# Weight, input and constant loads moved between the groups' transposing transfers, and four weight splits queued behind a normalisation chain

## The chip, the cores and the metric

The kernel runs on one core of a Trainium2 chip. A core has five engines, each with its own queue of instructions that it takes strictly in order: TensorE (PE, matrix products; its weight loads appear as PEld), VectorE (DVE), ScalarE (ACT), GpSimd (POOL) and SyncE (SP), which here only issues DMA transfers. All transfers of this kernel are issued by SP and share 16 DMA engines. The metric is the device time of one execution in microseconds (us), as the median of several runs. The profile shows one further execution; its times are counted from the start of its span.

## The reference

The input x has 2048 rows (tokens) of 448 features, in float32. The output is the sum of three things:

```python
xn  = layernorm(x)
out = x + A(xn) + B(xn)

def A(x):                       # a filter in the frequency domain
    return irfft2(rfft2(x) * (w_r + 1j * w_i))

def B(x):                       # token shift, then a channel MLP
    h  = gelu(layernorm(x) @ w1)             # w1: 448 x 448
    hs = shift(h) @ w2                       # four quarters of the features, shifted
    x1 = x + hs                              #   by +1, -1, +2, -2 tokens; w2: 448 x 448
    return x1 + gelu(layernorm(x1) @ w3) @ w4   # w3: 448 x 1792, w4: 1792 x 448
```

## The kernel before

Matrix products in float32 precision are made of float16 halves: a number is split into a high half (written by ACT) and a low half (the rest, written by DVE), and a product takes three passes (high by high, high by low, low by high). The weights are scaled first by a power of two that is worked out from the sum of their squares (`squares` on ACT, `powers` on PE and DVE), and then split (`split_w`, lines 258-261).

**Tokens.** The 2048 tokens lie in 16 blocks of 128 rows; block b holds every sixteenth token, so that a shift by a token is a step to the neighbouring block. The blocks are worked in four groups of four: `GRP = [[14, 15, 0, 1], [2, 3, 4, 5], [6, 7, 8, 9], [10, 11, 12, 13]]`. In this document they are the first to the fourth group (g = 0 to 3 in the code).

**The first stage**, up to about 115 us, does for each group, in this order:

- `load_x(g)` (line 190): two transfers of 448 KB bring the group's x.
- `norm1(g)` (lines 292-344): DVE takes statistics of the four blocks, then a chain of small DVE instructions gives scale and bias (the last of them writes `nm`, line 306), then the four blocks are scaled, each by POOL, ACT or DVE as the list `apply` says.
- `T1(g)` (line 741, `transpose_split` at 356): PE transposes the blocks with 16 products, ACT and DVE write the halves `xT`.
- `w1_unit` (408), four times: 11 products with w1, GELU on ACT, high half `hs` on ACT (line 417), low half on DVE (line 418), and a *transposing DMA* from SP (line 421) that writes the block's `h` with features on partitions. The buffers `hs` are four, used in turn (for the fourth group three), so that the halves of the next group can be written only when the transposing transfers of the group before have read theirs.
- `w2_tile(b)` (425), four times: 12 products of `h` with w2. Tile b takes `h` of the blocks b-1, b+1, b-2 and b+2, so that it needs blocks of the neighbouring groups too. The products with w2's low half need what DVE writes at line 260.
- `ln2` (442): the second normalisation of pairs or fours of blocks. It ends with a transposing DMA of its own (line 473) into `x2mem`.

**The second stage** (`mlp`): `front` multiplies with w3 (22 products of 256 columns each), ACT and DVE make halves `hf`; `back` multiplies them with w4 into `acc`. The first `mlp([0])` starts while the last tiles of the first stage run; the frequency filter (lines 870-909) runs beside the others. The matrices `w3raw` (four parts of 896 KB, the last part in two transfers of 448 KB to 64 partitions each) and `w4raw` (four transfers, inside `x2mem`) are needed for their squares, and then for their splits. The constants `csm` (643 KB) are first read by the filter's products at line 523.

**What sets the order.** The program text gives dependencies and wishes; a planner of the framework, when the kernel is built, lays down the order of each engine's queue. `with behind(key)` (line 349) tells the planner that an instruction is to be issued after those remembered in `after[key]`: `("h", g, i)` is the transposing DMA of block i of group g, `("a1",)` the last halves of the second group's transposition, `("a2",)` those of the third's. A further rule of the framework concerns SP: each DMA also waits until the eighth DMA before it has landed.

The order of SP's queue in the first stage of the kernel before: x of the first group, w1, x of the second, w2, x of the third and the fourth, all of w3, csm; then the four transposing transfers of the first group, four of the second, four loads of w4, four of the third group, four transfers of line 473, four of the fourth group.

Of the kernel before, what the change touches and what calls it, by code (L numbers as in the profile page):

```python
# [16 lines left out]
ALU = mybir.AluOpType  # L17
# [102 lines left out]
def body(tc, nc, x, wf, w1, w2, w3, w4, c_g, c_n, c_small, out):  # L120
    V, A, P, T, SY = nc.vector, nc.scalar, nc.gpsimd, nc.tensor, nc.sync
# [28 lines left out]
    def bank(tag, name):  # L150
        return ps.tile([128, 512], F32, tag=tag, bufs=2, name=name)
# [38 lines left out]
    def load_x(g):  # L190
        for b0 in sorted(GRP[g])[::2]:
            SY.dma_start(xt[b0 // 2], xv[:, b0:b0 + 2])
# [8 lines left out]

    load_x(1)
    SY.dma_start(w2s[:112], w2.rearrange("(k p) n -> p k n", p=112))
    for g in (2, 3):
        load_x(g)
    w3raw = pa.tile([128, 4, F], F32, tag="R", bufs=1, name="w3raw")

    def load_w3(ts):
        for t in ts:
            if t < 3:  # L210
                SY.dma_start(w3raw[:, t], w3[128 * t:128 * t + 128])
            else:
                for h in range(2):
                    SY.dma_start(w3raw[64 * h:64 * h + 64, 3], w3[384:448])

    load_w3(range(4))
    x2mem = pw.tile([128, 9 * F], F16, name="x2mem")
    x2all = x2mem[:, 0:8 * F].rearrange("p (j t n) -> p j t n", j=4, t=7)
    w4raw = x2mem.bitcast(F32)[:, F:].rearrange("p (f n) -> p f n", f=14)
# [3 lines left out]
    def load_w4(i):  # L223
        SY.dma_start(w4raw[:, W4F[i]:W4F[i + 1]], w4v[:, W4F[i]:W4F[i + 1]])

    csm = pc.tile([128, 2 * (256 + 2 * DF + 452 + 128)], F16, name="csm")
# [13 lines left out]
    def powers(m, n, key, tag="acc"):  # L240

        t = pc.tile([128, 2], F32, name=f"pt{key}")
        V.tensor_reduce(out=t[:, 0:1], in_=m[:, :n], axis=AX.X, op=ALU.add)
        pm = bank(tag, f"pm{key}")
        i = T.matmul(pm[:, 0:1], ones, t[:, 0:1], start=True, stop=True)
        after["p" + key] = (i.ins,)
        V.tensor_scalar(out=t[:, 1:2], in0=pm[:, 0:1], scalar1=2.0 ** -58, scalar2=None, op0=ALU.max)
        e = pc.tile([128, 3], I32, name=f"pe{key}")
        V.tensor_scalar(out=e[:, 0:1], in0=t.bitcast(I32)[:, 1:2], scalar1=1, scalar2=0x7F800000,
                        op0=ALU.logical_shift_right, op1=ALU.bitwise_and)  # L250
        V.tensor_scalar(out=e[:, 1:2], in0=e[:, 0:1], scalar1=-1, scalar2=185 << 23, op0=ALU.mult, op1=ALU.add)
        V.tensor_scalar(out=e[:, 2:3], in0=e[:, 0:1], scalar1=1, scalar2=69 << 23, op0=ALU.mult, op1=ALU.add)
        return e.bitcast(F32)[:, 1:2], e.bitcast(F32)[:, 2:3]
# [38 lines left out]
    def norm1(g, apply):  # L292

        bs = GRP[g]
        n, b0 = len(bs), bs[0]
        mv = pc.tile([128, 4, 2], F32, name=f"mva{b0}")
        stats([xb(b) for b in bs], f"a{b0}", mv)
        a = pc.tile([128, 2 * n], F32, name=f"va{b0}")
        yi = pc.tile([128, 2 * n], I32, name=f"vy{b0}")
        y = yi.bitcast(F32)  # L300
        V.tensor_scalar(out=a[:, n:], in0=mv[:, :n, 1], scalar1=1.0 + EPS, scalar2=EPS * EPS, op0=ALU.mult, op1=ALU.add)
        V.tensor_scalar(out=a[:, 0:n], in0=mv[:, :n, 1], scalar1=EPS, scalar2=None, op0=ALU.add)
        V.tensor_single_scalar(yi, a.bitcast(I32), 1, op=ALU.logical_shift_right)
        V.tensor_scalar(out=yi, in0=yi, scalar1=-1, scalar2=0x5F3759DF, op0=ALU.mult, op1=ALU.add)
        nm = pc.tile([128, n], F32, name=f"nma{b0}")
        V.scalar_tensor_tensor(out=nm, in0=mv[:, :n, 0], scalar=-1.0, in1=y[:, n:], op0=ALU.mult, op1=ALU.mult)
        for k, b in enumerate(bs):
            y_, m_ = y[:, n + k:n + k + 1], nm[:, k:k + 1]
            if apply[k] is A:
                A.activation(out=xb(b), in_=xb(b), func=AF.Identity, scale=y_, bias=m_)  # L310
            else:
                i = apply[k].tensor_scalar(out=xb(b), in0=xb(b), scalar1=y_, scalar2=m_, op0=ALU.mult, op1=ALU.add)
                if apply[k] is V:
                    after["n", g] = (i.ins,)

        q, z = (pc.tile([128, 2 * n], F32, tag=f"v{t}", bufs=2, name=f"v{t}{b0}") for t in "qz")
        w, r = (pc.tile([128, 2 * n], F32, name=f"v{t}{b0}") for t in "wr")
        nm1 = pc.tile([128, n], F32, name=f"nm{b0}")

        def refine():  # L320
            P.tensor_tensor(out=q, in0=y, in1=y, op=ALU.mult)
            P.tensor_tensor(out=q, in0=q, in1=a, op=ALU.mult)
            P.tensor_scalar(out=w, in0=q, scalar1=-10.0 / 3.0, scalar2=None, op0=ALU.add)
            P.tensor_tensor(out=w, in0=w, in1=q, op=ALU.mult)
            P.tensor_scalar(out=w, in0=w, scalar1=5.0, scalar2=None, op0=ALU.add)
            P.tensor_tensor(out=z, in0=w, in1=w, op=ALU.mult)
            P.tensor_tensor(out=z, in0=z, in1=q, op=ALU.mult)
            P.tensor_scalar(out=z, in0=z, scalar1=-0.5 * 0.375 ** 3, scalar2=1.5 * 0.375, op0=ALU.mult, op1=ALU.add)
            P.tensor_tensor(out=r, in0=z, in1=w, op=ALU.mult)
            P.tensor_scalar(out=gsc[:, 4 * g:4 * g + 4], in0=r[:, n:], scalar1=r1, scalar2=None, op0=ALU.mult)  # L330

        def scales():
            c, r1st, u = cs[:, 4 * g:4 * g + 4], w[:, 0:n], w[:, n:]
            P.tensor_tensor(out=r1st, in0=r[:, 0:n], in1=y[:, 0:n], op=ALU.mult)
            P.tensor_tensor(out=u, in0=r[:, n:], in1=r[:, n:], op=ALU.mult)
            P.tensor_tensor(out=c, in0=y[:, n:], in1=a[:, n:], op=ALU.mult)
            P.tensor_tensor(out=c, in0=c, in1=u, op=ALU.mult)
            P.tensor_tensor(out=c, in0=c, in1=r1st, op=ALU.mult)
            P.tensor_scalar(out=c, in0=c, scalar1=s12[:, 0:1], scalar2=None, op0=ALU.mult)
            P.tensor_tensor(out=nm1, in0=mv[:, :n, 0], in1=r1st, op=ALU.mult)  # L340
            P.tensor_scalar(out=nm1, in0=nm1, scalar1=-1.0, scalar2=None, op0=ALU.mult)
            for k, b in enumerate(bs):
                xn_scale[b], xn_bias[b] = r1st[:, k:k + 1], nm1[:, k:k + 1]
        return refine, scales

    after = {}

    @contextlib.contextmanager
    def behind(*key):
        key = key if len(key) > 1 else key[0]  # L350
        with contextlib.ExitStack() as st:
            for i in after[key]:
                st.enter_context(tc.issue_after(i))
            yield
# [53 lines left out]
    def w1_unit(g, i, pm=None):  # L408
        if pm is None:
            pm = bank(("mm", "mm", "acc", "acc")[i], f"pw1_{g}{i}")  # L410
            w1_in(g, i, pm, range(4))
        c = CS[GRP[g][i]]
        pm = pm[:, :D]
        pv_ = pm.rearrange("p (k n) -> p k n", k=4)
        h = hs_buf[c % (HS if g == 3 else HS + 1)]
        A.activation(out=pm, in_=pm, func=AF.Gelu_apprx_tanh, scale=gsc[:, c:c + 1])
        u = A.activation(out=h[:, 0, :, 0:112], in_=pv_, func=AF.Copy, scale=h1)
        v = V.scalar_tensor_tensor(out=h[:, 1, :, 0:112], in0=pv_, scalar=h1, in1=h[:, 0, :, 0:112],
                                   op0=ALU.mult, op1=ALU.subtract)
        o = h_at(g, i)  # L420
        d = SY.dma_start_transpose(out=hT[g][:, :, o:o + 128], in_=h.rearrange("p i k n -> p (i k n)"))  # L421
        after[g, i] = u.ins, v.ins
        after["h", g, i] = (d.ins,)
# [356 lines left out]
        T1(1, range(2, 4))  # L780
    for k in range(4):
        w1_unit(0, k, first[k])
    n1[1][0]()
    s12 = pc.tile([128, 4], F32, name="s12")
    V.tensor_tensor(out=s12[:, 0:1], in0=h1, in1=s2, op=ALU.mult)
# [2 lines left out]
    p12, eps12 = s12[:, 1:2], s12[:, 2:3]  # L788
    with behind("a1"):
        n1.append(norm1(2, [P, V, A, P]))  # L790
    with behind("a1"):
        for k in range(4):
            split_w(w2p[:, 0, k], w2p[:, 1, k], w2s[:112, k], s2[:112])
    h_alloc(1)
# [1 line left out]
        w1_unit(1, k)  # L796
    T1(2)
    with behind("h", 1, 3):
        for i in range(4):
            load_w4(i)  # L800
    n1[2][0]()
    for n in n1:
        n[1]()
# [2 lines left out]
    h_alloc(2)  # L806
    for k in range(4):
        w1_unit(2, k)
    for k in range(4):
        with behind(*((1, 3), ("a2",), ("a2",), (2, 0))[k]):  # L810
            squares(m3[:, k:k + 1], w3raw[:, k])
    s3, r3 = powers(m3, 4, "3", "mm")
    h3 = pc.tile([128, 1], F32, name="h3")
# [17 lines left out]
    h_alloc(3)  # L831
    for k in range(4):
        w1_unit(3, k)
    s4, r4 = powers(m4, 7, "4")
    p34 = pc.tile([128, 2], F32, name="p34")
    V.scalar_tensor_tensor(out=p34[:, 1:2], in0=r3, scalar=2.0 ** 5, in1=r4, op0=ALU.mult, op1=ALU.mult)
# [17 lines left out]
    for b in range(12, 16):  # L854
        w2_tile(b)
    ln2(range(12, 16), [P, A, P, A])
    SY.dma_start(csm, c_small)
    close("p1")
    close("pr")

# [76 lines left out]
```

## Time and profile before

| What | Value |
|---|---|
| median of 3 runs | 427.64 us (427.53 to 428.42) |
| the profiled execution | 432.02 us |
| its span, from the first instruction to the last | 430.2 us |
| PE busy | 413.0 us, 96% of the span |
| DVE, ACT, POOL busy | 294.8, 249.2, 109.9 us |
| moved by DMA | 47.61 MB |

The profile names a group of instructions by the line of the kernel, the engine, the operation and the tiles (output, then inputs). Matrix products are pipelined: a product's own duration is longer than the distance from one to the next, so that PE can be shown as busy and still lose time; the number of products in a stretch, times their distance when they follow each other closely, tells more than the busy time. "SPq" is SP issuing a transfer. In a timeline, what stands in brackets is the time for which the engine sat idle before the instruction and what ended it. In a table of stretches the columns are the length, then for each engine its busy time with the number of instructions, then the granted clock of TensorE as a share of full speed, the busy share of the DMA engines and the bytes moved.

### The profile page before, as it was taken

The page shows a single profiled execution, that of the slowest core. Times are in us where ns is not written, and L with a number is a line of the kernel's source. Part 1 is how long each engine was busy: PE and PEld are TensorE (multiplying, and loading weights), DVE is VectorE, ACT ScalarE, POOL GpSimd, SP SyncE. Part 2 cuts the span into 40 slices and gives each one's busy share as a digit, 9 for nine tenths or more (in the row PEclk, how much of TensorE's full clock was granted, in tenths as well). Part 3 has the DMA queues.
Part 4 walks back from the last instruction along what each step waited for, and adds up shares of the span by engine and source line. Part 5 has one row for each costly group of instructions (what it writes and reads, how often), then busy time and mean ns, then how long its engine had stood idle before and what let it go on. Part 6 is the DMA issues. An engine that isn't in the chain of part 4 may idle for free.

```text
span 430.2 us, 8446 instructions
## 1 busy us (share of the span) xinstructions
PE 413.0 (96%) x3289; PEld 288.0 (67%) x3289; DVE 294.8 (69%) x619; ACT 249.2 (58%) x428; POOL 109.9 (26%) x191
## 2 busy tenths in 40 slices
PE   7987999999998999999999999999999999999994
PEld 3543654666657777777778888787676767576772
DVE  4885799899756567663478889865999529942211
ACT  4685598974765867553387888864544414423221
POOL 2442270100223963420022211210454203200000
PEclk9998999999999999999999999999999999999998
DMA  8999926321755337223146565520001003431001
GB/s 279 366 267 182 308 50 109 75 52 35 182 105 110 87 122 265 89 86 98 38 115 159 152 160 151 139 73 8 2 2 64 23 2 129 148 111 43 2 0 44
DMA packets 51688, 47.61 MB, mean 111 GB/s; under 512 B 33920, under 2 KB 46912, under 8 KB 51648
## 3 DMA queue, kind: packets, MB, share of 16 engines
q1 hardware_dynamic: 51648, 47.07, 41.0%
q8 instruction: 26, 0.43, 0.4%
q14 instruction: 14, 0.11, 0.1%
HBM read 35.52 MB, written 3.67 MB: 91 GB/s over the span
## 4 chain that ended last, share of the span: by engine, by line
PE 49%; DVE 20%; ACT 9%; DMA 8%; issue 7%; SPq 3%; POOL 3%; ACTq 0%; DVEq 0%; POOLq 0%
PE pw L372 20%; PE acc L696 18%; PE pw L437 4%; ACT te L602 3%; PE ps L523 2%; DMA x2mem<-y 2%; SPq L421 2%; PE pw L398 2%; DVE te L604 1%; ACT zb L613 1%; DVE w4p L260 1%; DMA xr<-x 1%; DMA out<-xr 1%; DMA w1s<-w 1%; DVE pf L588 1%
## 5 line engine op out<-in xcount | busy, mean ns | idle before, releaser
L372 PE MATMUL pw<-x2mem,w3p 128*128 128x256 f16 x1232 | 152.0, 273 | 0.0
L696 PE MATMUL acc<-w4p,hf 128*128 128x448 f16 x672 | 139.9, 352 | 2.1 <-DVE hf L684 1.5
L372 PEld LDWEIGHTS <-w3p 128*128 128x128 f16 x1232 | 118.9, 98 | 24.4 <-issue 0.9
L696 PEld LDWEIGHTS <-hf 128*128 128x128 f16 x672 | 65.1, 98 | 53.4 <-DVE hf L684 2.3
L684 DVE SCALAR_TENSOR_TENSOR hf<-pw,h,hf 128x512 f16<-128x512 f32 x56 | 41.8, 748 | 57.9 <-ACT hf L683 57.5
L681 ACT ACTIVATE pw<-pw,pe 128x512 f32<-128x512 f32 x56 | 36.7, 656 | 68.2 <-PE pw L372 67.1
L437 PE MATMUL pw<-w2p,h 112*128 112x448 f16 x192 | 41.8, 363 | 2.9 <-DMA h<-hs 2.4
L683 ACT ACTIVATE hf<-pw,h 128x512 f16<-128x512 f32 x56 | 38.4, 687 | 1.5
L398 PE MATMUL pw<-w1p,xT 128*128 128x448 f16 x176 | 34.8, 352 | 1.5 <-ACT xT L365 0.8
L606 POOL TENSOR_TENSOR z<-te 128x450 f32<-128x450 f32 x16 | 16.3, 1018 | 74.0 <-DVE te L604 74.0
L437 PEld LDWEIGHTS <-h 112*128 112x128 f16 x192 | 18.9, 100 | 20.3 <-DMA h<-hs 3.7
L398 PEld LDWEIGHTS <-xT 128*128 128x128 f16 x176 | 17.0, 98 | 17.8 <-ACT xT L365 1.1
L653 POOL TENSOR_TENSOR e<-e 128x226 f32<-128x226 f32 x16 | 13.9, 867 | 56.5 <-ACT e L650 45.3
L587 ACT ACTIVATE pf<-pp 64x450 f16<-64x450 f32 x32 | 17.3, 542 | 16.6 <-DVE pf L588 8.1
L588 DVE TENSOR_TENSOR pf<-pp,pf 64x450 f16<-64x450 f32 x32 | 19.9, 622 | 5.3 <-ACT pf L587 5.0
L650 ACT ACTIVATE e<-pe 128x452 f32<-128x452 f32 x16 | 8.7, 548 | 15.6 <-DVE vh L661 12.3
L602 ACT ACTIVATE te<-px 64x450 f32<-64x450 f32 x32 | 17.3, 540 | 0.5
L660 ACT ACTIVATE vh<-e 128x448 f16<-128x448 f32 x16 | 9.2, 575 | 13.9 <-DVE e L658 8.3
L503 POOL TENSOR_TENSOR xr<-xf 128x452 f32<-128x452 f32 x8 | 9.7, 1207 | 27.0 <-issue 22.6
L506 POOL TENSOR_TENSOR f<-xr 128x452 f32<-128x452 f32 x16 | 16.1, 1029 | 0.6
L514 DVE TENSOR_TENSOR xh<-f,xh 128x452 f16<-128x452 f32 x16 | 11.8, 777 | 6.2 <-ACT xh L513 6.2
L668 PE MATMUL py<-vh,csm 128*128 128x448 f16 x48 | 13.5, 352 | 1.5 <-DVE vh L661 0.7
(155 smaller groups left out, 599.2 us busy)
## 6 DMA issues: line engine op xcount, KB each, us to landing
wc<-wf SPq DMA_DIRECT2D x32, 225.0 KB, 3.7
wl<-wf SPq DMA_DIRECT2D x8, 450.0 KB, 3.6
xt<-x SPq DMA_DIRECT2D x8, 448.0 KB, 8.1
xf<-x SPq DMA_DIRECT2D x8, 448.0 KB, 3.9
w3raw<-w SPq DMA_DIRECT2D x3, 896.0 KB, 13.6
xr<-x SPq DMA_DIRECT2D x12, 224.0 KB, 2.6
out<-xr SPq DMA_DIRECT2D x12, 224.0 KB, 1.9
gn<-c_g SPq DMA_DIRECT2D x16, 128.0 KB, 3.3
```

What stands on the lines that cost most here:

```text
L372: T.matmul(ps_out, wp[:, wi + t, cols], xT[:, xi + t, tok], start=t == 0 and wi + xi == 0, stop=t == 3 and wi == 4)
L398: T.matmul(pm[:, :D], xTs[g][:, xi + t, 128 * i:128 * i + 128], w1p[:, wi + t], start=t == 0 and wi + xi == 0, stop=t == 3 and wi == 4)
L437: T.matmul(pm[:, :D], hT[g][:112, 4 * hi + k, o:o + 128], w2p[:, wi, k], start=n == 0, stop=n == 11)
L506: P.tensor_tensor(out=f[:, :, k:k + 2].rearrange("p b s d -> p s b d"), in0=u[:, :, 0], in1=u[:, :, 1], op=op)
L587: A.activation(out=hi, in_=src, func=AF.Copy)
L588: V.tensor_tensor(out=lo, in0=src, in1=hi, op=ALU.subtract)
L602: A.activation(out=e[64 * h:64 * h + 64], in_=px_[64 - 64 * h:128 - 64 * h, :2 * DF], func=AF.Copy)
L606: P.tensor_tensor(out=z, in0=t[:, 0], in1=t[:, 1], op=ALU.add)
L681: A.activation(out=pm, in_=pm, func=AF.Gelu_apprx_tanh, scale=r3)
L683: i = A.activation(out=h[:, 0], in_=pm, func=AF.Copy, scale=h3)
L684: j = V.scalar_tensor_tensor(out=h[:, 1], in0=pm, scalar=h3, in1=h[:, 0], op0=ALU.mult, op1=ALU.subtract)
L696: m = T.matmul(acc[G][i][:, :D], h[:, hi, o:o + 128], w4p[0][:, wi, f], start=f == 0 and n == 0, stop=f == 13 and n == 2)
```

## The change

Eight places change. The order that comes out of the planner for SP's queue is then: x of the first group, w1, x of the second, w2, x of the third, the first two parts of w3; four transposing transfers of the first group; x of the fourth group, the third part of w3; four transposing transfers of the second group; the last part of w3 (two transfers), two loads of w4; four transposing transfers of the third group; two loads of w4; two transfers of line 473 and three of the fourth group; two of line 473; the last of the fourth group; csm. The work of no engine is added to or taken away, but since the planner starts from other times, the queues of PE, ACT, DVE and POOL differ up to the first products of the second MLP pass; after that all queues are in the same order as before.

```diff
-    for g in (2, 3):
-        load_x(g)
+    load_x(2)
...
-    load_w3(range(4))
+    load_w3([0, 1])
...
-        V.scalar_tensor_tensor(out=nm, in0=mv[:, :n, 0], scalar=-1.0, in1=y[:, n:], op0=ALU.mult, op1=ALU.mult)
+        i = V.scalar_tensor_tensor(out=nm, in0=mv[:, :n, 0], scalar=-1.0, in1=y[:, n:], op0=ALU.mult, op1=ALU.mult)
+        after["c", g] = (i.ins,)
...
+    with behind("h", 0, 3):
+        load_x(3)
+        load_w3([2])
...
-    with behind("a1"):
+    with behind("a1"), behind("c", 2):
         for k in range(4):
             split_w(w2p[:, 0, k], w2p[:, 1, k], w2s[:112, k], s2[:112])
...
     with behind("h", 1, 3):
-        for i in range(4):
-            load_w4(i)
+        load_w3([3])
+        load_w4(0)
+        load_w4(1)
...
+    with behind("h", 2, 3):
+        load_w4(2)
+        load_w4(3)
     for k in range(4):
-        with behind(*((1, 3), ("a2",), ("a2",), (2, 0))[k]):
+        with behind(*(("a2",), ("a2",), (2, 0), (2, 1))[k]):
             squares(m3[:, k:k + 1], w3raw[:, k])
...
+    with behind("h", 3, 3):
+        SY.dma_start(csm, c_small)
...
-    SY.dma_start(csm, c_small)
```

In the order of the changed kernel's queues, `split_w` of w2 lies as follows: its four instructions on DVE stand behind the third group's `nm`, its four on ACT stand where they stood. PE's queue has one product of the first `w2_tile` in the middle of the second group's products with w1, and it takes the third group's transposition and the first 14 of its products with w1 ahead of the first product that reads the second group's `h`; in the kernel before, that transposition lies among the first four tiles, whose products read that `h`, and the products with w1 lie behind them.

## The prediction

> **What bounds the kernel now.** I read the page first, then the table of stretches, then the timelines of PE, SP and DVE where PE loses time.
>
> ```profile
> span 430.2 us, 8446 instructions
> PE 413.0 (96%) x3289; PEld 288.0 (67%) x3289; DVE 294.8 (69%) x619; ACT 249.2 (58%) x428; POOL 109.9 (26%) x191
> ```
>
> PE is busy for 96% of the span. Since busy times of products overlap, I take their distances instead, from two dense pieces of the chain that ended last:
>
> ```profile
> 73.13 5.68 PE pw L398 x30
> 81.08 5.79 PE pw L372 x53
> ```
>
> A product of 448 columns takes 5.68/30 = 0.189 us, one of 256 columns 5.79/53 = 0.109 us. With these, the stretches in which PE loses time between 34 and 132 us are found (the first row of the table is for the loads, below):
>
> ```profile
> 0.00:20.00 20.00, 17.40 (x85) 8.66 (x85) 12.98 (x42) 10.88 (x21) 7.25 (x30) 1.00 0.94 314
> 34.00:38.50 4.50, 1.72 (x9) 0.44 (x8) 2.20 (x7) 2.82 (x5) 0.00 (x0) 1.00 1.09 215
> 38.50:42.00 3.50, 3.50 (x10) 1.46 (x11) 1.57 (x6) 2.96 (x4) 1.94 (x5) 0.52 1.13 189
> 66.00:70.00 4.00, 3.42 (x21) 1.66 (x20) 3.97 (x10) 3.09 (x5) 0.00 (x0) 1.00 0.71 133
> 125.00:132.00 7.00, 5.14 (x31) 2.62 (x30) 5.28 (x9) 3.86 (x8) 4.21 (x4) 1.00 0.52 99
> ```
>
> From 34 to 38.5 us PE issues 9 products, 9 x 0.189 = 1.7 us of work in 4.5: 2.8 lost. In the next 3.5 us the granted clock is 0.52 and 10 products (1.9 us of work) fill them: 1.6 lost. From 66 to 70 us 0.6 is lost, from 125 to 132 us 1.9. Together 6.9 us. PE's timeline names what it waited for:
>
> ```profile
> 26.11 8.12 PE L398 MATMUL pw<-w1p,xT 128*128 128x448 f16 x42 [0.25 <-DVE xT L366]
> 35.75 0.74 PE L437 MATMUL pw<-w2p,h 112*128 112x448 f16 x3 [1.52 <-DMA h<-hs]
> 38.49 4.67 PE L437 MATMUL pw<-w2p,h 112*128 112x448 f16 x15 [0.58 <-DMA h<-x2mem]
> 49.86 8.49 PE L398 MATMUL pw<-w1p,xT 128*128 128x448 f16 x44
> 86.70 1.87 PE L437 MATMUL pw<-w2p,h 112*128 112x448 f16 x9
> 128.94 0.93 PE L696 MATMUL acc<-w4p,hf 128*128 128x448 f16 x4 [0.61 <-ACT hf L683]
> 131.23 1.12 PE L696 MATMUL acc<-w4p,hf 128*128 128x448 f16 x5 [1.24 <-DVE hf L684]
> ```
>
> The first stall is for the first group's transposing transfers. Why they are late is seen at SP, in its timeline, in the landing times of the first of them alone, of all of them, and of the four loads of w4, and in the page's line of csm:
>
> ```profile
> 16.72 0.34 SPq L857 DMA_DIRECT2D csm<-c_small x1
> 23.96 11.12 SPq L421 DMA_TRANSPOSE h<-hs x3
> 42.15 2.68 SPq L224 DMA_DIRECT2D x2mem<-w x4
> ...
> DMA to landing us min/median/max: 10.8/10.8/10.8
> ...
> DMA to landing us min/median/max: 3.0/3.2/10.8
> ...
> DMA to landing us min/median/max: 5.3/8.2/10.7
> ...
> csm<-c_small SPq DMA_DIRECT2D x1, 643.0 KB, 17.2
> ```
>
> The first one, issued at 23.96, lands 10.8 us later, at 34.8, where 3.2 is the median; SP itself is held for 11 us over three issues. The loads ahead add up to 9.6 MB (8 x 448 KB of x, 784 of w1, 784 of w2, 3,584 of w3, 643 of csm), and the first 20 us move 314 GB/s: they need 31 us, and csm, the last of them, lands at 16.72 + 17.2 = 33.9. So the wait is for loads that nobody needs yet.
>
> **The first group's transfers.** In the changed order 6 x 448 + 784 + 784 + 2 x 896 KB lie ahead of them, 6.2 MB, which the first 20 us move (314 x 20 = 6.3 MB). The queue is empty when the first is issued at 23.96. It and the next two land 3.2 us after their issue, at 27 to 31 us; the fourth follows its low half on DVE (next part). PE's queue now has one product of the first tile behind 14 of the second group's (two of these lie ahead of the 42 above), so at 26.1 + 12 x 0.189 = 28.4. It needs block 15, whose transfer is issued 1.5 us after the first and lands at 28.7: 0.3 us of new stall. The second group's products then end at 34.5 (34.2 before).
>
> **DVE: w2's low halves behind the third group's chain.**
>
> ```profile
> 28.59 2.21 DVE L284 BATCH_NORM_STATS2 sta<-xt 128x6 f32<-128x448 f32 x4
> 30.71 1.27 DVE L260 SCALAR_TENSOR_TENSOR w2p<-w2s,pe,w2p 112x448 f16<-112x448 f32 x2
> 31.89 0.69 DVE L418 SCALAR_TENSOR_TENSOR x2mem<-pw,h,x2mem 128x448 f16<-128x448 f32 x1
> 35.54 0.69 DVE L418 SCALAR_TENSOR_TENSOR hs<-pw,h,hs 128x448 f16<-128x448 f32 x1 [1.49 <-ACT hs L417]
> 40.01 0.16 DVE L306 SCALAR_TENSOR_TENSOR nma<-mva,vy 128x4 f32<-128x4 f32 x1
> 34.88 0.63 ACT L417 ACTIVATE hs<-pw,h 128x448 f16<-128x448 f32 x1 [2.27 <-DMA h<-hs]
> ```
>
> Before, the chain's statistics end at 30.8, but `nm` is written at 40.2: the w2 halves stand ahead, then DVE waits for ACT, which waits for the first transposing transfer to have read its `hs` buffer. Changed: the fourth `hs` half at 30.8 to 31.4 (its transfer lands at 34.6), the chain's nine small instructions to 32.5 (0.09 to 0.2 us each), 7.7 us earlier. Then three w2 halves (0.63 each, from 1.27 for two), one block's scaling (0.5), the fourth: 35.5. What queues behind them are the second group's low halves: they start at 35.5, as before. So the second group's transfers are issued from 36.2 on, 0.7 after the first low half starts, about where they were. The delayed w2 halves are first read at about 34.8 and later; the first ends at 33.1, each further one ahead of its product.
>
> **Third group instead of waiting.** With `nm` at 32.5 its blocks are scaled by 34.9. PE has from 34.5 on: 11 products of the first group's `h`, the 16 transpositions (1.97 us for 16 by the row below) and 14 products with w1, 2.1 + 2.0 + 2.6 = 6.7 us, to 41.2, before a product needs the second group's `h`.
>
> ```profile
> 22.51 1.97 PE L362 MATMUL pta<-ident,xt 128*128 128x128 f32 x16 [0.65 <-POOL xt L312]
> ```
>
> **Loads put between.** x of the fourth group and a part of w3 (1.8 MB, 5.9 us at 314 GB/s) are queued behind the transfer that lands at 34.6 and ahead of those issued from 36.2: these land from about 41.4 on (40.5, and 0.9 for the transfer itself, as between csm and the first one). PE needs block 2 at 41.2: 0.2 to 0.3 us of stall. Bounds: 3.2 us from issue (39.4, no stall) and 10.8 (47.0, 5.8 us). I take the sum of bytes. The third group's first transfer is issued at about 47.5 (20 products after 41.4 PE has its first two blocks, at 45.2; GELU and the halves take some 2 us), lies behind 2.7 MB and lands at about 54. PE needs it 75 products and 12 transpositions after 41.4, at 57: hidden. The loads' own readers: the fourth group's x is read by DVE after the third group's `xT` halves, at about 40 (lands at 37.5); the third part of w3 by ACT after the third group's first half, at 47 (40.5); the last, two transfers of 448 KB behind the second group's, by ACT after the second half, at 50 (about 48.6); w4 and csm later, with over 5 us to spare. Each is covered by ACT's and DVE's earlier work; uncovered, ACT's queue and through it the w3 splits on DVE would move one for one.
>
> So to the middle of the stage PE gets back 2.8 + 1.6 (no gap, no half clock) + 0.6 and pays 0.3 + 0.3.
>
> **The fourth group.** Before, its first low half, the transfer and PE's use read:
>
> ```profile
> 81.55 0.66 DVE L418 SCALAR_TENSOR_TENSOR hs<-pw,h,hs 128x448 f16<-128x448 f32 x1
> 82.27 5.86 SPq L421 DMA_TRANSPOSE h<-hs x4
> ```
>
> Landing at 82.27 + 3.2 = 85.5, use at 86.70: 1.2 us in hand. In the changed queue PE has 31 instead of 53 products with w3 ahead of that use, 22 x 0.109 = 2.4 us less cover. If DVE gets there earlier by as much as PE does, PE stalls 2.4 - 1.2 = 1.2 us. DVE can: it has the same work, and between 34 and 48 us it was busy for 6.6 us only:
>
> ```profile
> 34.00:48.00 14.00, 11.22 (x57) 5.92 (x56) 6.56 (x16) 7.84 (x14) 5.20 (x20) 0.88 1.07 235
> ```
>
> **The loss at 125 to 132.** ACT reaches the `hf` half late there, because it waits in front of it for a `y` buffer that a transfer of line 473 has not yet read:
>
> ```profile
> 113.86 1.48 SPq L493 DMA_DIRECT2D xf<-x x3
> 115.64 3.98 SPq L473 DMA_TRANSPOSE x2mem<-y x2
> 122.75 0.67 ACT L459 ACTIVATE y<-xt,nm 128x448 f32<-128x448 f32 x1 [3.59 <-DMA x2mem<-y]
> ```
>
> These two transfers are queued behind three loads of x for the filter. In the changed order both pairs of line 473 go out ahead of these loads, so the 1.9 us go; late next is DVE with `hf`, for which I keep 0.5.
>
> **Sum.** Back: 2.8 + 1.6 + 0.6 + 1.9 = 6.9. Paid: 0.3 + 0.3 + 1.2 + 0.5 = 2.3. Net 4.6. After that all queues are in the old order, and PE is dense, so the shift stays. The span becomes 425.6, the execution 432.0 - 4.6 = 427.4; the runs' median stands 4.4 below the profiled execution, and I take the same difference off it: 427.64 - 4.6 = 423.0.
>
> **Rivals.**
> - *Nothing new stalls* (0.08): the whole 6.9 comes back, 420.7. Against it: the fourth group has too little cover.
> - *VectorE becomes the bound* (0.19). From 57 to 93 us it has hardly a free moment (it was 7 us idle before 48 and moves only by 4.6), and tiles wait for it to empty PSUM banks: the loss at 125 to 132 stays (1.9) and 0.5 more is lost: 425.4.
> - *Loads too late* (0.06). The last part of w3 behind the second group's transfers lands 10.7 us after its issue at 41.9, as the last of w4 did: 52.6 instead of 50. ACT, then the w3 splits and the fourth group are 2.6 later: 425.6. The Trainium skill, DMA: Bandwidth & Descriptors, Rules for kernel authors, speaks against the change here: it says to issue a DMA early and wait for it late, so that its fixed cost overlaps. The trace of before shows what early issue costs others, 10.8 us for a transfer behind the loads.
> - *Slower* (0.10). The second group's transfers, now behind loads, take 10.8 us as the first group's did: PE waits from 41.2 to 47.0, 5.8 us, and the half clock after a gap costs its 1.6 again: 423.0 - 0.3 + 5.8 + 1.6 = 430.1. It decides once they land after about 44.3, 8 us after issue (3.1 of stall and 1.6 for the clock use up the 4.6).
> - *No effect* (0.03): the stalls only move, 427.6.
>
> My forecast has 0.54. From 421 to 425 is its own range; with VectorE as the bound and the late loads the range is 420.4 to 426.4. Faster by over 0.2%, which is about what a measurement of this kernel can tell from no change (the three runs spread by 0.2%): 0.86; within it 0.04; slower 0.10.
>
> **What would show it.** The first transposing transfer lands near 27, not 34.8; no half clock near 40; the third group's products with w1 begin near 38 instead of 49.86; `nm` of that group near 32.5; the first use of the fourth group's `h` near 80 to 82, with a wait of about 1 us for DMA; no wait for `hf` near 125. Wrong would be: PE waiting over 3 us for `h` near 41, or DVE late with line 439 so that PE waits for banks between 57 and 95.

## The result, and the profile after

The changed kernel takes 426.27 us (median of 15 runs, 424.62 to 428.35), beside 428.31 for the kernel before in the same series; the ratio is 0.9945, with a 95% interval of 0.9923 to 0.9967. It is faster, by about 0.55% where 1.1% (427.64 to 423.0) was forecast; the medians differ by 2.0 us where 4.6 were forecast. 426.27 lies inside the forecast's wide range, above its own 421 to 425. The profiled execution took 428.35 us, 2.1 more than the median.

Top of the page of the changed kernel, then its table of stretches (length; busy time and instructions of PE, PEld, DVE, ACT and POOL; granted clock; DMA share; GB/s):

```profile
span 426.6 us, 8457 instructions
PE 412.9 (97%) x3289; PEld 288.1 (68%) x3289; DVE 291.7 (68%) x619; ACT 248.6 (58%) x428; POOL 107.8 (25%) x191
```

```profile
34.00:38.50 4.50, 4.34 (x27) 2.56 (x26) 4.27 (x8) 3.73 (x8) 4.07 (x8) 1.00 1.02 282
38.50:42.00 3.50, 3.50 (x23) 2.00 (x21) 3.02 (x5) 3.40 (x5) 2.15 (x11) 1.00 1.48 221
42.00:49.00 7.00, 4.82 (x18) 2.05 (x17) 3.93 (x16) 2.02 (x4) 1.79 (x5) 0.76 1.07 153
66.00:70.00 4.00, 4.00 (x23) 2.07 (x22) 4.00 (x11) 4.00 (x6) 0.00 (x0) 1.00 0.83 210
```

From 34 to 42 us PE is now nearly full. But from 42 to 49 it issues 18 instructions in 7 us, at a granted clock of 0.76: the gap and the half clock have moved some 7 us back. The timelines of DVE, PE and SP show the way there:

```profile
32.90 0.16 DVE L305 SCALAR_TENSOR_TENSOR nma<-mva,vy 128x4 f32<-128x4 f32 x1
32.98 1.87 DVE L259 SCALAR_TENSOR_TENSOR w2p<-w2s,pe,w2p 112x448 f16<-112x448 f32 x3
```

```profile
38.94 0.55 PE L398 MATMUL pw<-w1p,xT 128*128 128x448 f16 x2
...
44.38 2.51 PE L437 MATMUL pw<-w2p,h 112*128 112x448 f16 x9 [2.19 <-DMA h<-hs]
...
83.55 1.87 PE L437 MATMUL pw<-w2p,h 112*128 112x448 f16 x9
...
125.39 2.07 PE L696 MATMUL acc<-w4p,hf 128*128 128x448 f16 x10 [0.47 <-DVE hf L684]
```

```profile
24.47 4.57 SPq L421 DMA_TRANSPOSE h<-hs  x3
...
34.34 1.30 SPq L210 DMA_DIRECT2D w3raw<-w  x1
36.49 8.02 SPq L421 DMA_TRANSPOSE h<-hs  x3
```

The third group's `nm` comes at 32.90 instead of 40, its products with w1 begin at 38.94 instead of 49.86, as forecast. Then PE waits 2.19 us for the second group's `h`. The first of those transfers was issued at 36.5, behind x of the fourth group and the third part of w3; this answer on the transposing transfers issued from 35.5 to 37 us has its time from issue to landing:

```profile
DMA to landing us min/median/max: 7.8/7.8/7.8
```

The first group's first transfer, by the same view, took 3.4 us (10.8 before), as forecast. Up to here one would say: the second group's transfers took the gain back. A second profile of both kernels, below, shows that this is only half of it.

### The profile page after: what moved, and what is told of

Its sections match the earlier page's. It is cut to its first block, busy times and chain, and to the rows that moved or that the text cites. A ratio compares the mean times of both kernels' runs of the same rounds, so it can differ in the third digit from the quotient of the medians.

```text
span 426.6 us, 8457 instructions
## 1 busy us (share of the span) xinstructions
PE 412.9 (97%) x3289; PEld 288.1 (68%) x3289; DVE 291.7 (68%) x619; ACT 248.6 (58%) x428; POOL 107.8 (25%) x191
## 4 chain that ended last, share of the span: by engine, by line
PE 54%; DVE 8%; issue 3%; DMA 3%; ACT 1%; POOL 1%; DVEq 0%; SPq 0%
PE pw L372 22%; PE acc L696 22%; PE ps L523 3%; PE pu L625 2%; PE pp L580 2%; PE px L597 2%; DMA xr<-x 2%; DVE xt L669 1%; DMA out<-xr 1%; DVE xr L480 1%; DVE vh L661 1%; DVE e L657 1%; DVE x2mem L480 1%; DVE e L655 1%; DVE U L638 1%
## 5 line engine op out<-in xcount | busy, mean ns | idle before, releaser
L398 PE MATMUL pw<-w1p,xT 128*128 128x448 f16 x176 | 36.4, 360 | 1.4 <-ACT xT L365 0.8
L416 ACT ACTIVATE pw<-pw,gsc 128x448 f32<-128x448 f32 x16 | 9.3, 606 | 10.7 <-POOL xt L312 5.7
```

The costliest lines, as they stand in the source:

```text
L398: T.matmul(pm[:, :D], xTs[g][:, xi + t, 128 * i:128 * i + 128], w1p[:, wi + t], start=t == 0 and wi + xi == 0, stop=t == 3 and wi == 4)
```

## The experiments

All ratios are to the kernel before, run beside on the same chip, with 95% intervals. "Lost PE time" is the distance between the starts of successive products beyond the one that their columns need in dense stretches (0.187 us for 448 columns, 0.107 for 256), summed over a stretch of the trace. How small an excess is counted moves such a sum by up to 0.4 us, and the difference of two sums by some 0.3.

**The two halves of the change, one at a time.** First the w2 halves (the four DVE instructions that write w2's low halves) alone behind the third group's chain (the two edits below added to the kernel before, all loads where they were):

```diff
+        after["c", g] = (i.ins,)
...
-    with behind("a1"):
+    with behind("a1"), behind("c", 2):
         for k in range(4):
             split_w(...)
```

> The kernel before with one part of the change: VectorE's halves of w2 behind the third group's chain; all loads where they were. The first group's transfers still land from 34.8 on. PE's queue has the products that need them ahead of most of the third group's transposition, so it still waits from 34.2 to about 38.4, with 6 products and 2 transpositions inside; the third group's scale is there near 32.5 and its products with w1 can follow soon after 40. Theory 'the transfers are what PE waits for': ratio 0.998 to 1.002, the gap and the half clock near 38 to 42 remain. Theory 'the chain is what counts': ratio near 0.9945, as the whole change.

Measured: 423.84 us, ratio 0.9916 (0.9888 to 0.9944). The theory that the late transfers are what costs (about 1.000) fell: by its median the half that moves no load is ahead even of the whole change (0.9945), though the two intervals overlap. Its PE timeline:

```profile
35.93 0.36 PE L438 MATMUL pw<-w2p,h 112*128 112x448 f16 x1 [1.61 <-DMA h<-hs]
36.71 1.12 PE L438 MATMUL pw<-w2p,h 112*128 112x448 f16 x5 [0.42 <-DMA h<-hs]
...
80.22 1.87 PE L438 MATMUL pw<-w2p,h 112*128 112x448 f16 x9
...
124.42 0.92 PE L697 MATMUL acc<-w4p,hf 128*128 128x448 f16 x4
125.17 0.27 PE L373 MATMUL pw<-x2mem,w3p 128*128 128x256 f16 x1
125.28 1.68 PE L697 MATMUL acc<-w4p,hf 128*128 128x448 f16 x8
```

The first group's transfers are as late as before (10.3 us from issue to landing) and PE still waits for them, 1.61 and 0.42 us. But with `nm` at 32.48 the third group fills the time behind, and nothing is lost near 80 and 125. Why nothing is lost near 125 is most likely told by SP and ACT:

```profile
111.75 1.85 SPq L494 DMA_DIRECT2D xf<-x  x3
118.30 5.27 SPq L474 DMA_TRANSPOSE x2mem<-y  x4
```

```profile
113.46 0.67 ACT L460 ACTIVATE y<-xt,nm 128x448 f32<-128x448 f32 x1 [1.15 <-DMA x2mem<-y]
```

No edit touches these transfers, but the planner, which starts from other times, leaves four of the sixteen behind the filter's loads of x, where the kernel before leaves six. ACT's last wait for a `y` buffer ends at 113.46; in the kernel before it ends at 122.75, with the `hf` that is late behind it in ACT's queue. The changed kernel and all other variants have this order of SP's queue too.

Then the rest of the change alone, that is the moved loads and the later squares of w3 (the changed kernel without `behind("c", 2)`); its label and the forecast for it call this the loads alone:

> The changed kernel without the moved w2 halves: these stand ahead of the third group's chain again, the loads are as changed. The first group's transfers land from 27.9 on; the third group's scale comes near 35 instead of 33, its transposition starts near 37.5. PE waits about 1 us there, but by 42 it waits for the second group's transfers in any case. Theory 'loads are the change': ratio 0.994 to 0.998. Theory 'only both together': ratio 0.999 to 1.002.

Measured: 426.82 us, ratio 0.9972 (0.9952 to 0.9993). The w2 halves alone bring 0.84%, the rest alone 0.28%, both together 0.55% and, in a second series, 0.63%. By these figures the rest takes back some 0.2 to 0.3 points of what the w2 halves bring; since the intervals overlap, the ratios alone do not show it, and the traces have to say what is lost and where. That was the next question.

**What lies between the first and the second group's transfers.** Nothing there (x of the fourth group up front; w3's last two parts and one load of w4 behind the second group's transfers, three loads of w4 behind the third's); in part, against the changed kernel:

```diff
-    with behind("h", 0, 3):
-        load_x(3)
-        load_w3([2])
...
-        load_w3([3])
+        load_w3([2, 3])
```

> The changed kernel, but with nothing loaded between the first and the second group's transposing transfers: x of the fourth group goes in front of w3's first two parts, the third part of w3 goes behind the second group's transfers with the fourth part and one quarter of w4, the other three quarters behind the third group's. Theory 'loads between': in the changed kernel the second group's transfers land at 44.3 because x and w3 (1.8 MB) lie ahead of them, PE stands idle for 2.35 us at 42 and then runs 3.4 us at half clock (1.7 us). Without these loads the transfer issued near 36.5 lands near 39.6, PE waits at most 1 us near 39, no half clock between 30 and 60: about 3 us less than the changed kernel, ratio to before 0.986 to 0.990. Rival 'late by themselves' (the transposing transfers of the second group are slow for another reason): landing near 44 again, ratio 0.9945.

Measured: 425.54 us, ratio 0.9957 (0.9925 to 0.9989). The second group's first transfer lands at 39.2 and PE waits for none of them, yet the time is that of the changed kernel. The lost time has only moved; ACT's and PE's timelines:

```profile
48.94 1.70 ACT L238 ACTIVATE x2mem<-w3raw 128x1792 f16<-128x1792 f32 x1 [1.53 <-DMA w3raw<-w]
...
52.97 1.70 ACT L238 ACTIVATE x2mem<-w3raw 128x1792 f16<-128x1792 f32 x1 [0.67 <-DMA w3raw<-w]
```

```profile
83.39 1.88 PE L438 MATMUL pw<-w2p,h 112*128 112x448 f16 x9 [0.82 <-DMA h<-hs]
...
126.91 1.69 PE L697 MATMUL acc<-w4p,hf 128*128 128x448 f16 x8 [1.36 <-DVE hf L685]
```

ACT waits for the parts of w3, PE for the fourth group's `h` and for `hf`. The second variant exchanges the part of w3 between the transfers for a load of w4, so that two parts of w3 come later (against the changed kernel):

```diff
     with behind("h", 0, 3):
         load_x(3)
-        load_w3([2])
+        load_w4(0)
...
-        load_w3([3])
-        load_w4(0)
+        load_w3([2, 3])
```

> The changed kernel with one load swapped: between the first and the second group's transfers goes a quarter of w4 (896 KB, in rows of 1,792 bytes) instead of the third part of w3 (896 KB, in rows of 7,168 bytes); that part of w3 goes behind the second group's. Theory 'bytes': the same bytes ahead, the second group's first transfer lands near 44.3 again, the same gap of 2.35 us and the half clock, ratio 0.994 to 0.995. Theory 'slow w3 part': in the changed kernel that part took 4.8 us (38.5 to 43.3) where others took 2.2 to 2.4; if it is w3's rows that are slow beside queued transposing transfers, w4's quarter lands near 41, the transfers near 42, the gap shrinks under 1 us, no half clock: 2.5 to 3.5 us less than the changed kernel, ratio 0.986 to 0.989.

Measured: 429.18 us, ratio 1.0027 (1.0002 to 1.0052): slower than the kernel before, and outside both forecasts. Near 42 it went as the theory of the slow w3 part has it: w4's quarter lands at 41.3, the first transposing transfer at 42.1, and nothing is lost there. But in the second profile of the changed kernel (below) w3's part lands at 40.4, so its rows alone are not what made it late. ACT and PE:

```profile
50.95 1.70 ACT L237 ACTIVATE x2mem<-w3raw 128x1792 f16<-128x1792 f32 x1 [3.43 <-DMA w3raw<-w]
...
55.03 1.70 ACT L237 ACTIVATE x2mem<-w3raw 128x1792 f16<-128x1792 f32 x1 [1.28 <-DMA w3raw<-w]
```

```profile
54.62 2.24 PE L437 MATMUL pw<-w2p,h 112*128 112x448 f16 x11 [1.17 <-DVE xt L439]
```

ACT stands 3.43 us before one square of w3, with the third group's halves queued behind it, and PE loses 3.2 us between 50 and 70. So the forecast's rival "loads too late" is real when two parts of w3 come late, in a stronger form than it was given. The sentence of the Trainium skill that was set beside it (DMA: Bandwidth & Descriptors, Rules for kernel authors: issue early, wait late) fits these two runs.

**Both kernels profiled once more.** The first profile of the kernel before took 432.02 us, 4.4 above its median. That asked for a second one.

> The kernel before, profiled once more. Theory A: the profiled execution on which the sum was made (432.02 us, clock 0.993) is one of the minority with a low granted clock: of 35 executions of this kernel, the 10 with a clock of 0.996 or less have a mean of 429.6 us, the other 25 one of 427.6. Then another execution has no half clock between 38 and 42 us, a shorter end after its last product (about 4 us instead of 5.9), and a time near 427.6; the gap at 34 to 38 us stays, some 2.5 us. Theory B: the half clock near 38.5 belongs to this kernel's gap: it is there again, and the time is 429 to 432.

Measured: 427.56 us, near the medians of this kernel (427.5 to 428.3 in five series). Its page, stretches and chain of waits, and from the first profile of the same kernel the step that answers to the last of these lines:

```profile
span 425.8 us, 8446 instructions
```

```profile
34.00:38.50 4.50, 2.29 (x11) 0.83 (x11) 2.27 (x6) 3.46 (x7) 0.00 (x0) 1.00 1.03 193
38.50:42.00 3.50, 3.38 (x22) 2.00 (x20) 2.12 (x5) 2.32 (x3) 2.46 (x7) 1.00 1.26 189
```

```profile
417.71 4.55 PE acc L696 x24
```

```profile
420.10 4.55 PE acc L696 x24
```

Between 38.5 and 42 the clock is 1.00 and PE issues 22 instructions, not 10 at 0.52. The gap before it is there too, 2.4 us. And behind the last 24 products the first profile had 430.2 - 424.65 = 5.6 us, this one 425.8 - 422.26 = 3.5. So 2 us of the first profile's surplus lie at its end, and the rest is the half clock and its neighbourhood. Over 80 executions of the kernel before, 25 had a mean granted clock of 0.997 or less and took 429.6 us on average, the other 55 took 427.6.

> The changed kernel once more. Theory A: the second group's first transposing transfer lands late each time, behind the loads, but by a varying amount: between 42 and 45 us, so PE waits 0.5 to 3 us near 42; a half clock follows only in some executions (2 of 15 had a clock of 0.996 or less). A time of 425 to 427 and a ratio of 0.994 to 0.997. Theory B (the prediction's): the landing at 44.3 was an accident, this profile shows 41.4 and a time of 423 to 424.

Measured: 425.74 us, ratio 0.9937 (0.9914 to 0.9961); of the 24 executions of this kernel in both series, 2 had such a low clock. The profiled one took 425.74, its median. Its page, PE's and ACT's timelines, and the first transfer of the second group from issue to landing:

```profile
span 423.8 us, 8457 instructions
```

```profile
41.42 1.88 PE L437 MATMUL pw<-w2p,h 112*128 112x448 f16 x9
...
80.30 1.88 PE L437 MATMUL pw<-w2p,h 112*128 112x448 f16 x9 [0.87 <-DMA h<-hs]
...
122.34 2.07 PE L696 MATMUL acc<-w4p,hf 128*128 128x448 f16 x10 [0.28 <-DVE hf L684]
```

```profile
51.48 1.70 ACT L237 ACTIVATE x2mem<-w3raw 128x1792 f16<-128x1792 f32 x1 [2.01 <-DMA w3raw<-w]
```

```profile
DMA to landing us min/median/max: 5.6/5.6/5.6
```

Issued at 35.80 and landed 5.6 us later, at 41.4, as in the forecast; PE starts at 41.42 without a gap. My expectation of another late landing fell, and so did theory B's time of 423 to 424. The landing scatters between executions, 5.6 and 7.8 us with the same loads ahead. In both it comes 1.0 us behind the landing of w3's part (40.4 here, 43.3 in the first profile), so it is the load ahead that scatters, and PE, which needs the block at 41.4 to 41.8, pays for each tenth.

Now two profiles that lie near their medians can be compared. Lost PE time in us:

| stretch, us | before, first profile | before, again | changed, first profile | changed, again | w2 halves alone |
|---|---|---|---|---|---|
| 20 to 30 | 2.25 | 2.14 | 2.70 | 2.42 | 2.35 |
| 30 to 50 | 4.99 | 3.05 | 4.41 | 0.45 | 2.55 |
| 50 to 70 | 1.02 | 0.99 | 0.14 | 0.34 | 0.14 |
| 70 to 100 | 0.14 | 0.14 | 0.14 | 1.57 | 0.14 |
| 120 to 135 | 2.21 | 2.07 | 1.24 | 1.06 | 0.00 |
| everything else | 7.98 | 7.78 | 8.45 | 8.33 | 7.54 |
| sum | 18.59 | 16.17 | 17.08 | 14.17 | 12.72 |

Before again to changed again the sum falls by 2.0 us and the span by 2.0; the medians fall by 2.0 in the first series and 2.5 in the second. In the first profile of the changed kernel the fourth group's stall is missing: PE comes to it 4.1 us later than in the second profile, after the 4 us lost near 42, and `h` lands only 2.7 us later.

The last column shows where the w2 halves alone gain 3.45 us on the kernel before: 0.5 between 30 and 50, 0.85 between 50 and 70, and 2.07 between 120 and 135, behind the other order of SP's queue. So the larger part of the gain does not arise near the third group's chain.

**Single pieces on top of the w2 halves.** First csm late and nothing else (`SY.dma_start(csm, c_small)` behind the fourth group's transfers, as in the change), then the squares late and nothing else:

> The kernel before with the w2 halves behind the third group's chain, and one load alone moved: csm, to behind the fourth group's transposing transfers. Theory A (loads ahead of the first transposing transfers cost what they take in bytes): 643 KB less, about 2 us at 314 GB/s, the first transfers land near 32.5 instead of 34.3, PE's waits of 1.77 and 0.59 us near 35 shrink to about 0.5, ratio to the kernel before 0.987 to 0.990. Theory B (an early gap is made good later, since DVE and ACT set the pace of the third and fourth group): no change against the w2 halves alone, 0.991 to 0.993.

Measured: 423.42 us, ratio 0.9891 (0.9858 to 0.9924). The first group's first transfer lands 7.5 us after issue, at 31.5 instead of 34.3, and PE's waits shrink to these:

```profile
35.92 0.44 PE L363 MATMUL pta<-ident,xt 128*128 128x128 f32 x2 [0.46 <-POOL xt L313]
...
39.53 1.88 PE L438 MATMUL pw<-w2p,h 112*128 112x448 f16 x9 [0.50 <-DMA h<-hs]
```

Its ratio is as theory A has it, but its interval reaches theory B's as well; the trace speaks for A, with 1.3 us less lost between 30 and 50 than with the w2 halves alone. Fewer bytes ahead bring an earlier landing, as the forecast had it, here 2.8 us for 643 KB. The size is loose: the first transfer lands at 34.0 to 35.7 in the four profiles with csm ahead, at 31.5 and 32.3 in the two without.

```diff
-        with behind(*((1, 3), ("a2",), ("a2",), (2, 0))[k]):
+        with behind(*(("a2",), ("a2",), (2, 0), (2, 1))[k]):
             squares(m3[:, k:k + 1], w3raw[:, k])
```

> The kernel before with the w2 halves behind the third group's chain and, in addition, the squares of w3 each one step later in ACT's order, as in the changed kernel; all loads as before. Theory A (the late loads take back the gain, not the order of the squares): as the w2 halves alone, ratio 0.990 to 0.993, no wait for hf near 125 us. Theory B (the later squares push ACT and DVE, and that brings the waits for hf near 125 us in the changed kernel): 0.994 to 0.997, with 1 to 2 us of waits there.

Measured: 425.26 us, ratio 0.9926 (0.9902 to 0.9951), so the ratio doesn't separate it from the w2 halves alone. The trace does separate it at the place in question (the profiled execution took 429.15 us, after a wait of 3.29 us for `h` near 37 and 6.8 us at the half clock):

```profile
129.96 1.69 PE L697 MATMUL acc<-w4p,hf 128*128 128x448 f16 x8 [0.93 <-DVE hf L685]
```

The wait for `hf` is back. All seven profiles with the squares one step later lose 0.8 to 2.2 us between 120 and 135, the five with the w2 halves behind the chain and the squares in the old place 0 to 0.4. That ties the loss to the squares' place, by association and this one pair; in one of the seven, the loads alone, most of it is waits for the filter's `xh` instead of `hf`.

Then the loads, one by one, on top of the w2 halves and csm late. The last part of w3 behind the second group's transfers:

> As the run with the w2 halves queued behind and csm late (0.9891), and w3's last part moved, as in the changed kernel, behind the second group's transposing transfers. Theory A (late parts of w3 hold ACT's squares, and through ACT and DVE the fourth group): ACT waits 1 to 2 us for w3raw near 50 us, PE waits about 1 us for the fourth group's h near 80, ratio 0.992 to 0.995. Theory B (the last part of w3 lands in time, the 0.9 MB fewer ahead of the first transposing transfers close the rest of the gap at 35 to 39 us, 1.2 us): 0.986 to 0.989.

Measured: 424.22 us, ratio 0.991 (0.9877 to 0.9943), between the two forecasts. The stall came, but one group earlier than I said, at the third group's `h`, whose first transfer took 9.9 us behind w3's part and w4; ACT's and PE's timelines:

```profile
50.12 1.70 ACT L238 ACTIVATE x2mem<-w3raw 128x1792 f16<-128x1792 f32 x1 [1.68 <-DMA w3raw<-w]
```

```profile
59.13 2.25 PE L438 MATMUL pw<-w2p,h 112*128 112x448 f16 x11 [1.46 <-DMA h<-hs]
```

x of the fourth group between the first and the second group's transfers:

> As the run with the w2 halves queued behind and csm late (0.9891), and x of the fourth group moved, as in the changed kernel, between the first and the second group's transposing transfers. Theory A (late parts of w3 are the cost, x is not: it lands near 38 and is read after 40): no stall near 80, the gap at 35 to 39 us closes, ratio 0.986 to 0.989. Theory B (any load between the groups' transfers delays the second group's, and PE waits near 42): a gap of 1 us or more there, 0.990 to 0.994.

Measured: 424.79 us, ratio 0.9942 (0.9915 to 0.9969). No gap near 35 to 42, as theory A had it, but the gain didn't come. PE's timeline has the wait at a place neither theory named:

```profile
29.80 0.36 PE L437 MATMUL pw<-w2p,h 112*128 112x448 f16 x1 [1.17 <-DMA h<-hs]
```

This is the single product of the first tile that the planner, told of early transfers, sets among the second group's products with w1. With 7,840 KB still ahead (in the changed kernel 6,048), the transfer it needs lands at 29.8. Bytes are not all of it: in the run with w3's last part late 7,840 KB lay ahead too, and the first transfer landed at 27.1 instead of 28.8. Theory A was right that x itself lands in time; the ratio is at the upper edge of theory B's range.

The last two loads of w4 behind the third group's transfers:

> As the run with the w2 halves queued behind and csm late (0.9891), and the last two loads of w4 moved, as in the changed kernel, behind the third group's transposing transfers. Theory A (late parts of w3 are the cost): no difference, 0.988 to 0.990, no wait for hf near 125. Theory B (w4's squares and splits come later and push ACT and DVE): waits for hf near 125 us of 1 to 2 us, 0.992 to 0.995.

Measured: 422.82 us, ratio 0.9881 (0.9846 to 0.9916). As theory A had it, moving these two loads costs nothing. This is the fastest version found; its interval lies below that of the changed kernel's first series (0.9923 to 0.9967). Its waits near 37 and 40 are 0.47 and 0.31 us; none is left near 80 and 125.

The changed kernel with all of w3 up front again:

```diff
-    load_w3([0, 1])
+    load_w3(range(4))
...
-        load_w3([2])
...
-        load_w3([3])
```

> The changed kernel with all of w3 up front again, so that only x of the fourth group lies between the first and the second group's transposing transfers; everything else as changed. Theory A (the late parts of w3 take back the gain): no wait for the fourth group's h near 80, ratio 0.988 to 0.992, against 0.9945 and 0.9937 for the changed kernel. Theory B (x, w4 or the order of the squares take it back): 0.993 to 0.996, with the waits near 80 and 125 as in the changed kernel.

Measured: 425.01 us, ratio 0.9932 (0.9904 to 0.996), which can't be told from the changed kernel. In its PE timeline the loss near 80 is gone, as theory A said, so w3's place is most likely what brought it (1.57 us in the second profile of the changed kernel, 0.14 here; the first profile of the changed kernel had 0.14 too, for the reason given above). But this stands in its place, and the squares' wait stays:

```profile
30.24 0.36 PE L437 MATMUL pw<-w2p,h 112*128 112x448 f16 x1 [1.54 <-DMA h<-hs]
...
125.39 1.69 PE L696 MATMUL acc<-w4p,hf 128*128 128x448 f16 x8 [0.64 <-DVE hf L684]
```

## Why the prediction was wrong, and where it was right

The direction and most of the steps held; the size, 4.6 us instead of about 2.0, did not. Term by term, in us, against two profiles that lie near their medians:

| step | forecast | measured |
|---|---|---|
| middle: gap 2.8 and half clock 1.6 back, 0.3 and 0.3 paid (20 to 50 us) | +3.8 | +2.3 |
| 66 to 70 | +0.6 | +0.65 |
| fourth group | -1.2 | -1.4 |
| `hf`: 1.9 back, 0.5 paid | +1.4 | +1.0 |
| everything else | 0 | -0.55 |
| sum | +4.6 | +2.0 |

- **The step that failed is the half clock's 1.6 us in "Back: 2.8 + 1.6 + 0.6 + 1.9", together with "The span becomes 425.6, the execution 432.0 - 4.6 = 427.4; ... I take the same difference off it".** The sum was made against one execution 4.4 us above the median, and the difference was carried over as if every execution had the stalls of that one. The half clock was a stall of that execution: the second profile has a clock of 1.00 there and loses 3.05 us between 30 and 50 where 4.4 were counted. A kernel can't win back at its median what its median doesn't lose. This alone is 1.4 of the missing 2.6 us. The warning stood in the numbers: three runs within 0.9 us of each other, and a profile 4.4 above them. Over the 80 executions the low clock costs some 0.6 us on average (25 of 80, 2.0 us each), not 1.6. Most of the rest is what is paid at `hf` (0.5 forecast, 1.06 measured) and 0.55 lost where the forecast has "PE is dense, so the shift stays".
- **The transfers.** First group: landing near 27 forecast, 27.9 and 27.1 measured. Second group: 41.4 forecast, 41.4 in one execution and 44.3 in the other, 2.35 us of lost time and the half clock behind it (4.05 together where 0.3 was taken). The rival "slower" described that mechanism, and its threshold of 44.3 was just reached. It decides in some executions, not in the median.
- **DVE and the third group.** `nm` at 32.9 and 32.2 (32.5 forecast), products with w1 at 38.9 and 38.3 (38). This step carries the change: alone it gives 0.84%. The forecast put the gain down to the first group's transfers ("the wait is for loads that nobody needs yet"). The runs say otherwise: without the w2 halves the moved loads and later squares give 0.28%, and with the w2 halves alone PE still waits 2 us for those transfers and yet loses less in the sum. The larger part of what the w2 halves bring arises, however, not where the third group fills the wait but near 125, most likely through SP's order near 112 us. That is the forecast's own account of the loss at 125 to 132, and none of the moved loads is needed for it.
- **The fourth group.** 1.2 forecast, 1.4 measured, near 80 as said. The cause given (31 instead of 53 products with w3 as cover) does not hold: the w2 halves alone have 24 of these products ahead of that use and no wait, and the run with nothing between the transfers has 59 and waits 0.82 us. So the size was right by luck. What feeds the stall is most likely ACT, 2 us late because the last part of w3 lands at 51.4. "About 48.6", hidden, was the estimate; the rival of the late loads had 52.6.
- **`hf` near 125.** The 1.9 came back, as said (2.07 lost before, none with the w2 halves alone). Forecast: 0.5 kept for DVE. Measured 1.06, DVE as named. The cause is not VectorE as the bound, since the w2 halves alone leave no wait there with the same DVE work, but most likely the place of the squares, which I had counted at nothing.
- **Everything else.** 0.55 us more is lost at later places, the most of it near 367 at an `hf` of DVE. All six profiles with x of the fourth group moved lose 0.7 to 1.2 us at this place, the other eight, the kernel before among them, 0.4. How that load reaches so far is not shown.

## What to carry to other kernels

Compare the profiled execution's own time with the runs' median before a sum is made on it: what lies between the two is no loss that a change can win back, and a second profile at the median is worth more than a finer sum. A load moved out of the way of one wait is queued in the way of the next: list its own reader, and every transfer behind it, with the landing that it then gets. Test the parts of a change one by one: here moving four instructions within one engine's queue gave 0.84%, more by its median than the whole change. Then look at every queue and not only at the one that was edited, since the planner had reordered another, and the larger part of the gain lay behind that.

## What the runs showed of the hardware

- Of two executions of one kernel with a similar gap on PE, one went on at the half clock and one did not: before, 2.8 us lost from 34 to 38.5 with a granted clock of 0.52 behind it, and 2.4 us lost with 1.00. The half clock also followed 2.35 us near 42 in the changed kernel (0.76 over the 7 us in which it lies). The Trainium skill (TensorE: Matmul & The Clock Gate, What's actually happening) gives an idle window of about 3.4 us for the fall and says that the window runs freely, so that the cost varies between runs. The variation agrees. The only gap of about that length, 3.3 us before 37.3 in the run with the late squares, came with 6.8 us at the half clock, which began inside it (0.52 from 36 to 37.3). That 2.35 us in the changed kernel were enough differs from the Trainium skill, and there the rows decide.
- A transposing transfer took 3.1 to 3.4 us with nothing ahead of it, and 5.6, 7.8, 9.9 and 10.3 us behind queued loads; with the same bytes ahead it differed by 2.2 us between two executions of the changed kernel, and in both it landed 1.0 us behind the load ahead of it.
